# First projection of a two-MLP kernel: 384-column products, taken product by product over all of DFF

## The chip, the cores and the metric

The kernel runs on one core of a Trainium2 chip. The metric is device time in microseconds, the median of a few executions. One execution was also taken with the hardware profiler; its rows are the rows of this document. Engines are called as the profile calls them: PE (TensorE matmul), PEld (TensorE weight load), DVE (VectorE), ACT (ScalarE), POOL (GpSimd) and SP, which here only issues transfers (DMA).

## The reference

```python
# linear attention: q, k, v are (8, 8, 576, 64)
q_s = softmax(q, axis=-1); k_s = softmax(k, axis=2)
kv = einsum('bhsd,bhse->bhde', k_s, v)
attn = einsum('bhsd,bhde->bhse', q_s, kv)
x = attn.transpose(0, 2, 1, 3).reshape(4608, 512)
# first MLP: 512 -> 2048 -> 512
h = x @ w_in;  r = max(h, 0);  y = (r * r) @ w_out
# second MLP: 512 -> 2048 -> 512
h = y @ w2_in; out = (max(h, 0) + alpha * min(h, 0)) @ w2_out
```

All four matrix products have 4608 tokens; DFF is 2048 and the model width is 512.

## The kernel before

**Four stages.** The hidden stage of the first MLP (with the attention woven in) runs on nine tiles of 512 tokens, matmul line L759. It stores the squared hidden values to DRAM (`r_dram[0]`, L780). The first projection, `project_stage`, reads them back (L809), and stores its result to `y_scratch` (L877). The hidden stage of the second MLP, `hidden_wide`, reads that (L942, L945), runs at line L983 and stores to `r_dram[1]` (L1046). The second projection is `project_stage` again (matmul line L796 for both projections, output store L881).

**Split operands.** Every float32 operand is split into a head and a rest of type float32r (`split`: head by ACT at L484, rest by DVE at L487). Each product of operands is three matmuls: rest times head, head times rest, head times head (`PAIRS`).

**Seven products for eight.** Both projections and the wide hidden stage use Strassen's scheme with Winograd's sums: a 2x2 block product is made from seven products, numbered 1 to 7, of blocks and of sums of blocks. The sums of the weights are made once, behind the first hidden stage, and parked in DRAM (`made`, store L461). They come back when their stage begins (`brought`, load L465), one group `g` (256 of the 2048 rows of DFF) at a time, 896 KB each, all seven blocks of the group together.

**`project_stage`.** For each tile of 512 tokens and each of eight groups `g`, `token_blocks` loads four blocks of 256 tokens by 128 rows of DFF, makes the three sums on DVE (L503, L509, L512; in the last tile two of them on POOL), and splits everything: three blocks at once (768 columns) and twice two sums (512 columns). The group then does its seven products, each six matmuls of 256 columns (`product`). Each of the seven products has a PSUM bank of its own, which is summed over the eight groups. When the tile ends, `combine` makes the four result blocks from the seven banks on ACT and DVE (L828, L835, L844).

**`hidden_wide`.** Tiles are four times 512 tokens wide per half (1024 tokens) and once 256. Here banks are reused: product 6 is added to product 1's bank after ACT has copied it out, and so on (the `read` table in `Group.product`), with the copies and sums between products (L1005, L1008, L1035, L1011).

**What sets the order.** Python code adds operations to a `Plan` with an engine, an estimated cost, what they come after, and which buffers they take new or use. `Plan.run` then picks, engine by engine, what is issued next (earliest due among those that can start), finds a place in the two big SBUF areas (`sb`, float32; `sr`, float32r) by each kind's list of homes and its quota, and so fixes the order of every engine's instructions. On the chip each engine runs its list in that order, and waits at its head.

Of the kernel before, what the change touches and what calls it, by code (L numbers as in the profile page):

```python
# [18 lines left out]
P = 128  # L19
TOK = 512  # L20
WORDS = (53 * 256, 168 * 256)
# [3 lines left out]
HALF = 256  # L25

# [217 lines left out]
def linear_attention_two_mlps(  # L244
# [34 lines left out]
    r_dram = [dram.tile([T, P, NF, TOK], F32, name=f"r{n}") for n in range(2)]  # L279
# [3 lines left out]
    y_dram = y_dram.rearrange("t p c (h n) -> t p (c h) n", h=2)  # L283
# [21 lines left out]
    early = dict(within=(63 * KB_ // 2, 53 * KB_))  # L305
    x_early = dict(area=1, within=(64 * KB_, 158 * KB_), top=True)

    def homes(first, step, n):
# [10 lines left out]
        kvw=kind(2 * P, 2 * KB + 2, area=1, homes=homes(158, 1, 10)),  # L319
        q=kind(2 * R * D, 2, **early), qe=kind(2 * R * D, 2, **early), ke=kind(2 * KR * D, 2, **early),  # L320
        km=kind(2 * D, 2, **early), m=kind(GRAIN, 2, **early), rs=kind(GRAIN, 2, **early),
        mx=kind(GRAIN, 2, **early), sm=kind(GRAIN, 2, **early), ro=kind(2 * BANK, 2, **early),
        qT=kind(2 * BANK, 2, **x_early), x=kind(2 * BANK, 2 * KB + 2, **x_early),
        ri=kind(7 * HALF, 3, homes=homes(14, 7, 3)), o=kind(BANK, 8, homes=homes(37, 2, 8)),
        xr=kind(7 * BANK, 2, homes=homes(14, 14, 2)), xt=kind(2 * BANK, 14, area=1, homes=homes(112, 4, 14)),
        z=kind(2 * BANK, 8, homes=homes(49, -4, 2) + homes(8, -4, 3) + homes(38, -4, 7)),
        w3=kind(6 * HALF, G, area=1, homes=homes(0, 14, G)), w4=kind(8 * HALF, G, area=1, homes=homes(6, 14, G)),
        r3=kind(6 * HALF, 4, area=1, homes=homes(112, 6, 4)), r4=kind(4 * HALF, 8, area=1, homes=homes(136, 4, 8)),
# [90 lines left out]

    class Pairs:  # L420


        def __init__(self, n, kd, w, hidden, brought_after, signed=None):

            self.blocks, self.sums, self.done = [], [], []
            for g in range(G):
                t, f = hidden(g)
                made = self.made(n, kd, w, g, h1[t, f], begun[t] + 12 * MM * f + MADE, signed)
                self.brought(n, g, [made, brought_after[g]])
# [42 lines left out]

        def operand(self, g, p):

            s, i = A_OF[p]
            return [self.blocks, self.sums][s][g].ap.rearrange("p (n i m) -> p n i m", n=2, m=HALF)[:, :, i], s
# [244 lines left out]
    def hidden_stage(xs, weights, activate, store, blocks):  # L721
# [3 lines left out]
        stored = {}  # L725
        for t in range(T):
# [22 lines left out]
            for f in range(NF):  # L749
# [51 lines left out]
    def project_stage(r, stored, weights, first, store, gate):  # L801

        last, stored_c = {}, {}
        for t in range(T):

            acc = {p: bank(K["acc"]) for p in ((1, 2, 3, 6, 7, 4, 5) if first or t < T - 1 else (1, 6, 7, 5, 2, 3, 4))}
            for g in range(NF // 2):
                def load(to, t=t, g=g):
                    nc.sync.dma_start(to.rearrange("p (f t) -> p f t", f=2), r[t, :, 2 * g:2 * g + 2, :])  # L809
                bufs, done = token_blocks(load, [*stored[t, g], gate], t == T - 1)  # L810
# [64 lines left out]
    def store_y(t, i, j, c):  # L875
        to = y_dram[t].rearrange("p (k c h) n -> p k c h n", c=2, h=2)[:, 2 - i, :, 2 - j]
        nc.sync.dma_start(to, c.rearrange("p (c t) -> p c t", c=2))  # L877

# [6 lines left out]
    WIDE = [(t, BANK) for t in range(0, T - 1, 2)] + [(T - 1, HALF)]  # L885

    def wide_blocks(load, after, n):
# [27 lines left out]
        loaded = None  # L915
        for h in range(2):
            loaded = plan.add(
                lambda h=h: load(block(0, 4).rearrange("p (k h t) -> p k h t", k=2, h=2)[:, :, h], h), "sp", ISSUE,
                [*after, loaded], new=[] if h else [j], use=[j], mb=n / 1000,
            )  # L920
# [12 lines left out]
    def hidden_wide(weights, y_done, r, gate):  # L933

        last, stored = {}, {}
        for t, (first, n) in enumerate(WIDE):
            xs = []
            for c in range(2):
                def load(to, h, c=c, first=first, n=n):
                    if n == BANK:  # L940
                        y = y_dram[first + h].rearrange("p (k c h) t -> p k c (h t)", c=2, h=2)
                        nc.sync.dma_start(to, y[:, :, c])  # L942
                    else:
                        y = y_dram[first].rearrange("p (k c h) t -> p k c h t", c=2, h=2)
                        nc.sync.dma_start(to, y[:, :, c, h])  # L945
                ys = [y_done[t2, i, j] for t2 in range(first, first + n // HALF) for i in (1, 2) for j in (1, 2)]
                xs.append(wide_blocks(load, [*ys, gate(t, last)], n))
            for g in range(0, G, 2):
                both = [Group(weights, xs, t, first, n, g + m, r) for m in range(2)]
                for m, p in ((0, 1), (1, 1), (0, 2), (0, 6), (1, 6), (1, 2), (0, 5), (0, 7), (1, 7), (1, 5), (0, 4), (1, 4), (0, 3), (1, 3)):  # L950
                    last[t, g + m] = both[m].product(p)
                for m in range(2):
                    for h in range(2):
                        for t2 in range(first, first + n // HALF) if n == HALF else [first + h]:
                            stored.setdefault((t2, g + m), []).append(both[m].stored[h])
        return last, stored

    class Group:


        def __init__(self, weights, xs, t, first, n, g, r):
            self.weights, self.xs, self.first, self.n, self.g, self.r = weights, xs, first, n, g, r
            self.banks, self.ends, self.stored = {}, {}, {}
            self.z = [buf(K["z"]), buf(K["z"])]
# [5 lines left out]
        def product(self, p):  # L970
# [7 lines left out]
            def unit():  # L978
                a, _ = self.weights.operand(g, p)
                for c in range(2):  # L980
                    b = self.xs[c][0][p].ap.rearrange("p (n t) -> p n t", t=BANK if n == BANK else n)
                    for i, (u, w) in enumerate(PAIRS):
                        nc.tensor.matmul(  # L983
                            h.ap[:, :n], a[:, u, c * P:(c + 1) * P], b[:, w, :n],
# [6 lines left out]
            us = MM if n == BANK else MM2  # L991
            o = product_op(
                unit, 6 * us / MM, [self.weights.done[g][s], *(x[1][p] for x in self.xs), self.ends.get(read)],
# [47 lines left out]
        def store(self, h, after, z):  # L1041
            n, g, first = self.n, self.g, self.first

            def fn():
                to = self.r[first + h, :, 2 * g:2 * g + 2, :] if n == BANK else self.r[first, :, 2 * g:2 * g + 2, h * n:(h + 1) * n]
                nc.sync.dma_start(to, z.ap[:, :2 * n].rearrange("p (f t) -> p f t", f=2))  # L1046

            self.stored[h] = plan.add(fn, "sp", ISSUE, after, use=[z], due=now[0] + 8.0, mb=n / 1000)
# [29 lines left out]
    w1o = Pairs(0, "o", w1_out, lambda g: (1 + g // 4, 4 * (g % 4)), [h1[T - 1, max(0, 2 * (g - 3))] for g in range(G)])  # L1078
    p1, y_done = project_stage(r_dram[0], r1, w1o, True, store_y, h1[T - 1, 8])
    w2i = Pairs(1, "i", w2_in, lambda g: (3 + g // 4, 4 * (g % 4)), [p1[T - 1, max(0, g - 2), 5] for g in range(G)])  # L1080
    h2, r2 = hidden_wide(w2i, y_done, r_dram[1], lambda t, h2: p1[T - 1, 3, 5] if t == 0 else h2[t - 1, 3])
    end = len(WIDE) - 1
    w2o = Pairs(2, "o", w2_out, lambda g: (5 + g // 4, 4 * (g % 4)), [h2[end, max(0, g - 2)] for g in range(G)], signed)
# [31 lines left out]
```

## Time and profile before

| | |
|---|---|
| median of 3 runs | 1604.04 us (1603.2 to 1604.18) |
| the profiled execution | 1603.52 us, its span 1601.7 us |
| PE, DVE, ACT, POOL busy | 98%, 74%, 52%, 8% of the span |
| granted PE clock | 0.996 of full over the span |
| first hidden stage, first projection, wide hidden stage, second projection | end at 522.0, 886.4, 1234.4 and 1601.7 us |

Busy time is the union of an engine's instructions. Matmuls overlap one another, so the time that one costs in a stream is the stretch divided by the count, not the mean duration of one. A stretch in which PE is busy throughout can only become shorter through fewer or cheaper matmuls; a gap in it belongs to whoever PE waited for.

### The profile page before, as it was taken

To read this page: it belongs to the slowest core of one execution; us is meant where nothing else is said; L and a number is where in the kernel's file an instruction comes from. 1 tells how busy PE (TensorE), PEld (TensorE's weight loads), DVE (VectorE), ACT (ScalarE), POOL (GpSimd) and SP (SyncE) were. 2 spreads that over 40 slices of the span, in tenths; PEclk is the share of its full clock that TensorE was granted. 3 is DMA by queue.
4 is the path that set the end of the run, shared out by engine and by line. 5 is a ranking of instruction groups with operands and counts; after the bars stand their busy time and mean duration, and the time that the engine had idled before them with its cause. 6 is when DMAs were issued, how large, how long until landed. Compare 5 with 4: busy or idle time off the path is not lost.

```text
span 1601.7 us, 27016 instructions
## 1 busy us (share of the span) xinstructions
PE 1563.7 (98%) x10496; PEld 1418.2 (89%) x10496; DVE 1193.0 (74%) x2058; ACT 829.2 (52%) x1352; POOL 133.9 (8%) x140
## 2 busy tenths in 40 slices
PE   4899999999999999999999999999999999999998
PEld 3678888888888999999999788888889999999998
DVE  6766666677634888888877877768578998888873
ACT  5676766766657644444444543434246544444442
POOL 4440212011100000000012000000000000000012
PEclk9999999999999999999999999999999999999999
DMA  8667778888658544444445442434327554444431
GB/s 211 199 205 264 271 236 277 278 264 279 247 201 287 174 138 138 133 131 132 132 132 211 171 158 115 174 115 175 128 109 263 194 162 133 145 140 129 131 121 62
DMA packets 128976, 286.99 MB, mean 179 GB/s; under 512 B 15184, under 2 KB 78672, under 8 KB 128848
## 3 DMA queue, kind: packets, MB, share of 16 engines
q1 hardware_dynamic: 128848, 285.27, 54.1%
q8 instruction: 82, 1.34, 0.4%
q14 instruction: 46, 0.38, 0.1%
HBM read 168.83 MB, written 116.39 MB: 178 GB/s over the span
## 4 chain that ended last, share of the span: by engine, by line
PE 94%; DMA 2%; DVE 2%; issue 1%; POOL 1%; ACT 1%; SPq 0%; DVEq 0%; POOLq 0%
PE bank L796 45%; PE bank L759 23%; PE bank L983 21%; PE bank L593 1%; DMA sb<-in_moe_w_in_dram 1%; PE bank L667 1%; DMA sb<-in_k_dram 1%; PE bank L739 1%; PE bank L682 1%; PE bank L683 1%; PE bank L681 0%; POOL sr L400 0%; DMA sb<-in_q_dram 0%; DVE sr L487 0%; DVE sb L1011 0%
## 5 line engine op out<-in xcount | busy, mean ns | idle before, releaser
L796 PE MATMUL bank<-sr 128*128 128x256 f32 x6048 | 726.6, 283 | 0.4 <-DVE sr L487 0.4
L796 PEld LDWEIGHTS bank<-sr 128*128 128x128 f32 x6048 | 726.1, 192 | 0.8 <-DVE sr L487 0.6
L484 ACT CAST sr<-sb 128x512 fp32r<-128x512 f32 (+2 forms) x480 | 337.1, 718 | 357.6 <-PE bank L796 212.7
L487 DVE TENSOR_TENSOR sr<-sb,sr 128x512 fp32r<-128x512 f32 (+2 forms) x480 | 380.7, 818 | 108.8 <-ACT sr L484 107.6
L759 PE MATMUL bank<-sr 128*128 128x512 f32 x1680 | 406.9, 397 | 5.4 <-POOL sr L400 5.4
L759 PEld LDWEIGHTS bank<-sr 128*128 128x128 f32 x1680 | 312.1, 190 | 72.3 <-POOL sr L400 7.1
L983 PE MATMUL bank<-sr 128*128 128x512 f32 (+1 forms) x1680 | 346.4, 368 | 2.1 <-ACT sr L909 1.3
L983 PEld LDWEIGHTS bank<-sr 128*128 128x128 f32 x1680 | 293.0, 188 | 55.3 <-ACT sr L909 1.8
L1005 ACT ACTIVATE sb<-bank,sign 128x512 f32<-128x512 f32 (+1 forms) x160 | 103.4, 648 | 194.9 <-PE bank L983 190.2
L787 ACT ACTIVATE sb<-bank 128x512 f32<-128x512 f32 x144 | 85.8, 596 | 75.5 <-PE bank L759 64.9
L1011 DVE SCALAR_TENSOR_TENSOR sb<-sb,al 128x512 f32<-128x512 f32 (+1 forms) x160 | 110.0, 697 | 11.4 <-ACT sb L1005 8.0
L509 POOL TENSOR_TENSOR sb<-sb 128x256 f32<-128x256 f32 x16 | 16.7, 1045 | 1097.8 <-ACT sr L484 1060.3
L503 DVE TENSOR_TENSOR sb<-sb 128x512 f32<-128x512 f32 x144 | 100.1, 695 | 1.5 <-DMA sb<-r 1.5
L835 DVE TENSOR_TENSOR sb<-sb,bank 128x512 f32<-128x512 f32 x108 | 71.3, 686 | 35.1 <-PE bank L796 15.4
L788 ACT ACTIVATE sb<-sb 128x512 f32<-128x512 f32 x144 | 91.3, 634 | 3.4
L1008 DVE SCALAR_TENSOR_TENSOR sb<-bank,sign,sb 128x512 f32<-128x512 f32 (+1 forms) x80 | 55.5, 694 | 41.8 <-PE bank L983 39.6
L512 DVE TENSOR_TENSOR sb<-sb 128x256 f32<-128x256 f32 x128 | 54.3, 424 | 4.0
L663 POOL TENSOR_TENSOR sb<-sb 128x512 f32<-128x512 f32 x36 | 37.9, 1053 | 228.9 <-DVE sb L659 103.5
L509 DVE TENSOR_TENSOR sb<-sb 128x256 f32<-128x256 f32 x128 | 53.9, 421 | 0.7
L689 DVE TENSOR_TENSOR sr<-bank,sr 128x512 fp32r<-128x512 f32 x36 | 24.8, 690 | 37.2 <-ACT sr L686 36.9
L566 DVE TENSOR_REDUCE sb<-sb 128x128 f32<-128x640 f32 x32 | 41.6, 1301 | 9.4 <-DMA sb<-in_k_dram 7.0
L1035 DVE SCALAR_TENSOR_TENSOR sb<-bank,sign,sb 128x512 f32<-128x512 f32 (+1 forms) x40 | 27.7, 697 | 27.8 <-ACT sb L1005 20.2
(68 smaller groups left out, 913.4 us busy)
## 6 DMA issues: line engine op xcount, KB each, us to landing
sb<-r SPq DMA_DIRECT2D x144, 512.0 KB, 3.7
r<-sb SPq DMA_DIRECT2D x136, 512.0 KB, 3.0
j<-sb SPq DMA_DIRECT2D x24, 896.0 KB, 5.8
sb<-j SPq DMA_DIRECT2D x24, 896.0 KB, 5.8
sb<-in_moe_w_in_dram SPq DMA_DIRECT2D x32, 512.0 KB, 5.2
sb<-in_moe_w_out_dram SPq DMA_DIRECT2D x32, 512.0 KB, 4.6
y_scratch<-sb SPq DMA_DIRECT2D x36, 256.0 KB, 2.6
out_dram<-sb SPq DMA_DIRECT2D x36, 256.0 KB, 2.6
```

What stands on the lines that cost most here:

```text
L484: nc.scalar.copy(of(parts.ap[:, :n]), what())
L487: nc.vector.tensor_tensor(of(parts.ap[:, n:]), what(), of(parts.ap[:, :n].bitcast(F32)), op=ALU.subtract)
L503: nc.vector.tensor_tensor(two(block(4, 2)), two(block(1, 2)), block(0).unsqueeze(1).to_broadcast([P, 2, HALF]), op=ALU.subtract)
L509: e.tensor_tensor(block(6), block(2), block(4), op=ALU.add)
L759: nc.tensor.matmul(h.ap, w[:, a, c, :], x_parts(x[c][0])[:, b, :], start=(c == 0 and n == 0), stop=(c == KB - 1 and n == 2),)
L787: o = plan.add(lambda: nc.scalar.activation(ro.ap[:, half], h.ap, AF.Relu), "act", 0.6, [o, even], new=new, use=[h, ro])
L788: return plan.add(lambda: nc.scalar.activation(ro.ap[:, half], ro.ap[:, half], AF.Square), "act", 0.63, [o], use=[ro])
L796: nc.tensor.matmul(target[:, m * HALF:(m + 1) * HALF], one[:, u, ms], two[:, w, :], start=start and m == 0 and i == 0, stop=stop and m == ...
L835: lambda: nc.vector.tensor_tensor(c.ap, b.ap, acc[p].ap, op=ALU.add), "dve", 0.7,
L983: nc.tensor.matmul(h.ap[:, :n], a[:, u, c * P:(c + 1) * P], b[:, w, :n], start=start and c == 0 and i == 0, stop=c == 1 and i == 2, skip_g ...
L1005: nc.scalar.mul(to, h.ap[:, :n], sign[:, by])
L1011: nc.vector.scalar_tensor_tensor(to, to, al[:, by], to, op0=ALU.mult, op1=ALU.max)
```

## The change

The first projection gets a stage of its own, `project_wide`. A tile is now 768 tokens, six tiles in all, and a block is 384 tokens wide. The loop is turned inside out: for each of the seven products (in the order 1, 2, 5, 6, 7, 4, 3) all eight groups of DFF are run through before the next product, for both halves `m` of the output rows, in one PSUM bank for each half. The bank is carried from product to product as in `hidden_wide`, so that results leave it by a copy on ACT and three sums on DVE for each half and tile (class `Side`). The weights come back by product instead of by group: seven loads of 1 MB (`brought_all`), 256 columns out of each group, and one split of 2048 columns each. The tokens come as sixteen loads of 384 KB for a tile, the sums are made in place (`combine`), and the operands of a product stand in four slots of which there are eight.

Around it: `r_dram` and `y_scratch` are laid out by partition, so that a store or load of 512 tokens has runs of 2 KB instead of 4 KB; the wide hidden stage has four tiles of 464 tokens per half and one of 448; the second projection has 7 instead of 8 buffers for its sums (`r4`); `ro`, the two store buffers of the first hidden stage, have fixed places; SBUF is divided anew.

```diff
-WORDS = (53 * 256, 168 * 256)
+WORDS = (57 * 256, 164 * 256)
+WIDE = 464
+THIRD = 384
...
-    r_dram = [dram.tile([T, P, NF, TOK], F32, name=f"r{n}") for n in range(2)]
+    r_dram = [dram.tile([P, NF, NT], F32, name=f"r{n}") for n in range(2)]
...
+        pp=kind(2 * DFF // 2, 2, homes=homes(16, 8, 2)), wp=kind(2 * DFF, 4, area=1, homes=homes(0, 16, 4)), wq=kind(2 * DFF, 3, area=1, homes=homes(64, 16, 3)),
+        rb=kind(2 * THIRD, 16, homes=homes(33, 3, 5) + homes(0, 3, 11)), tt=kind(4 * THIRD, 8, area=1, homes=homes(112, 6, 8)),
+        c=kind(THIRD, 6, homes=homes(48, 1.5, 6)),
...
-        r3=kind(6 * HALF, 4, area=1, homes=homes(112, 6, 4)), r4=kind(4 * HALF, 8, area=1, homes=homes(136, 4, 8)),
+        r3=kind(6 * HALF, 4, area=1, homes=homes(112, 6, 4)), r4=kind(4 * HALF, 7, area=1, homes=homes(136, 4, 7)),
...
+    ORDER = (1, 2, 5, 6, 7, 4, 3)
...
+            if self.by_product:
+                self.all, self.done, self.loads = {}, {}, []
+                for i in (4, 5, 6, 0, 1, 2, 3):
+                    self.brought_all(self.n, ORDER[i], K["wp" if i < 4 else "wq"], [*self.parts, after[i]])
...
+    def project_wide(r, stored, weights, gate):
...
+        for t in range(NT // (2 * n)):
...
+            bring(1)
+            operand(1, 1)
+            bring(3)
+            operand(2, 3)
+            bring(0)
+            combine(1, 1, 0, ALU.subtract)
+            operand(5, 1)
+            bring(2)
+            combine(1, 2, 1, ALU.add)
+            operand(6, 1)
+            combine(0, 2, 0, ALU.subtract)
+            operand(7, 0)
+            combine(3, 3, 1, ALU.subtract)
+            operand(4, 3)
+            operand(3, 2)
+            sides = [Side(weights, slots, split_done, t, t0, n, m, y_done) for m in range(2)]
+            for p in ORDER:
+                for part in range(2):
+                    for m in range(2):
+                        for q in (2 * part, 2 * part + 1):
+                            last[t, p] = sides[m].product(p, q)
...
+            read = {6: 1, 7: 6, 4: 7, 3: 5}.get(p) if q == 0 else None
...
-    WIDE = [(t, BANK) for t in range(0, T - 1, 2)] + [(T - 1, HALF)]
+    WIDES = [(2 * WIDE * t, min(WIDE, NT // 2 - WIDE * t)) for t in range(-(-NT // (2 * WIDE)))]
...
+    w1o.bring([h1[T - 1, max(0, 4 * (i - 1))] if i < 4 else h1[T - 2, 8] for i in range(7)])
...
+    p1, y_done = project_wide(r_dram[0], r1, w1o, lambda t, p1, b: [p1[t - 1, 5]] if t else w1o_gate[b])
```

How the order of instructions moves, at three places. In the changed kernel L805 is the old L759 (first hidden stage), L1007 the matmul of the new stage, L826 the store of `r` (old L780), L508 the load of a product's weights, L494 the old L465, L942 the token load of the new stage, L533 the old L487, L952 the sums of token blocks and L1030 the sums from the banks.

PE at the end of the first hidden stage, before:

```order
L759 MATMUL bank_70<-sr 128x512 x12
L759 MATMUL bank_68<-sr 128x512 x12
L759 MATMUL bank_69<-sr 128x512 x12
L796 MATMUL bank_72<-sr 128x256 x6
L796 MATMUL bank_65<-sr 128x256 x6
L796 MATMUL bank_66<-sr 128x256 x6
```

and after:

```order
L805 MATMUL bank_71<-sr 128x512 x12
L1007 MATMUL bank_69<-sr 128x384 x12
L1007 MATMUL bank_70<-sr 128x384 x12
L1007 MATMUL bank_69<-sr 128x384 x6
L805 MATMUL bank_72<-sr 128x512 x12
L805 MATMUL bank_68<-sr 128x512 x12
L805 MATMUL bank_67<-sr 128x512 x12
L805 MATMUL bank_66<-sr 128x512 x12
L1007 MATMUL bank_69<-sr 128x384 x6
L1007 MATMUL bank_70<-sr 128x384 x12
```

Before, the projection began when the last hidden row block was through; now thirty of its 384-column matmuls stand ahead of the last four row blocks, and wait there for their operands.

SP in the last tile of the first hidden stage, before (`r` are the stores of hidden values and the token loads, `j` the parked weights):

```order
L461 DMA j_77<-sb 128x1792
L780 DMA r_73<-sb 128x1024 x2
L465 DMA sb<-j_75 128x1792 x2
L780 DMA r_73<-sb 128x1024 x2
L465 DMA sb<-j_75 128x1792
L780 DMA r_73<-sb 128x1024
L465 DMA sb<-j_75 128x1792
L780 DMA r_73<-sb 128x1024
L809 DMA sb<-r_73 128x1024 x2
L465 DMA sb<-j_75 128x1792
```

and after:

```order
L508 DMA sb<-j_75 128x8x256 x2
L826 DMA r_73<-sb 128x2x512
L490 DMA j_77<-sb 128x1792
L826 DMA r_73<-sb 128x2x512
L508 DMA sb<-j_75 128x8x256
L826 DMA r_73<-sb 128x2x512 x2
L508 DMA sb<-j_75 128x8x256 x2
L826 DMA r_73<-sb 128x2x512 x2
L942 DMA sb<-r_73 128x2x384 x8
L508 DMA sb<-j_75 128x8x256
L826 DMA r_73<-sb 128x2x512 x2
L508 DMA sb<-j_75 128x8x256
```

All seven weight loads now stand here, in runs of 1 KB (256 floats), and eight token loads in runs of 1.5 KB; before, the group loads stood here one by one between the stores, in one run of 7 KB for each partition, with token loads in runs of 4 KB.

DVE in the middle of the first projection, before (one group is one L503, L509, L512 and three L487):

```order
L487 TENSOR_TENSOR sr<-sb,sr 128x768
L509 TENSOR_TENSOR sb<-sb 128x256
L512 TENSOR_TENSOR sb<-sb 128x256
L487 TENSOR_TENSOR sr<-sb,sr 128x512 x2
L503 TENSOR_TENSOR sb<-sb 128x512
```

and after, some half of a tile:

```order
L533 TENSOR_TENSOR sr<-sb,sr 128x768 x2
L1030 TENSOR_TENSOR sb<-bank_65,sb 128x384
L952 TENSOR_TENSOR sb<-sb 128x768 x2
L1030 TENSOR_TENSOR sb<-bank_71,sb 128x384
L533 TENSOR_TENSOR sr<-sb,sr 128x768 x2
L952 TENSOR_TENSOR sb<-sb 128x768
L533 TENSOR_TENSOR sr<-sb,sr 128x768 x2
L952 TENSOR_TENSOR sb<-sb 128x768 x2
L533 TENSOR_TENSOR sr<-sb,sr 128x768 x8
L1030 TENSOR_TENSOR sb<-bank_72,sb 128x384
```

All splits and sums of blocks have 768 columns now, and the sums from the banks are spread over the tile instead of standing at its end.

## Rows read from the trace of the kernel before

**Rows 1.** The page, part 1: engine, busy us (share of the span), instructions.
```profile
PE 1563.7 (98%) x10496; PEld 1418.2 (89%) x10496; DVE 1193.0 (74%) x2058; ACT 829.2 (52%) x1352; POOL 133.9 (8%) x140
```
**Rows 2.** The page, part 4: the chain that ended last, shares of the span.
```profile
PE 94%; DMA 2%; DVE 2%; issue 1%; POOL 1%; ACT 1%; SPq 0%; DVEq 0%; POOLq 0%
PE bank L796 45%; PE bank L759 23%; PE bank L983 21%; PE bank L593 1%; DMA sb<-in_moe_w_in_dram 1%; PE bank L667 1%; DMA sb<-in_k_dram 1%; PE bank L739 1%; PE bank L682 1%; PE bank L683 1%; PE bank L681 0%; POOL sr L400 0%; DMA sb<-in_q_dram 0%; DVE sr L487 0%; DVE sb L1011 0%
```
**Rows 3.** Windows by stage: from:to, length, busy us (instructions), clock, DMA share, GB/s.
```profile
0.00:28.00 28.00, 9.43 (x59) 6.11 (x60) 17.86 (x39) 11.99 (x21) 12.38 (x26) 1.00 0.81 201
522.00:886.40 364.40, 363.56 (x3027) 363.09 (x3026) 301.44 (x480) 168.81 (x252) 16.14 (x16) 1.00 0.47 146
886.40:1234.40 348.00, 346.32 (x1685) 293.40 (x1686) 261.83 (x396) 148.71 (x243) 0.00 (x0) 1.00 0.42 154
1234.40:1601.70 367.30, 362.42 (x3019) 362.02 (x3017) 298.87 (x486) 162.02 (x240) 15.65 (x17) 1.00 0.45 139
```
**Rows 4.** Waits of PE from 500 us on: us in total, times, longest.
```profile
PE bank L983 <- ACT sr L909: 1.3, 1, 1.3
PE bank L983 <- DVE sr L911: 0.8, 1, 0.8
PE bank L796 <- DVE sr L487: 0.4, 1, 0.4
```
**Rows 5.** Timeline of PE in the first projection: start, us, line, count.
```profile
529.75 350.44 PE L796 MATMUL bank<-sr 128*128 128x256 f32 x2919
```
**Rows 6.** The chain in order of time, last matmuls of the first hidden stage.
```profile
475.75 46.24 PE bank L759 x204
```
**Rows 7.** Groups by line and form, 900 to 1100 us: busy us, mean ns.
```profile
L983 PE MATMUL bank<-sr 128*128 128x512 f32 x884 | 200.5, 389 | 0.0
```
**Rows 8.** Groups by line and form, whole span, DVE and ACT.
```profile
L487 DVE TENSOR_TENSOR sr<-sb,sr 128x768 fp32r<-128x768 f32 x168 | 160.7, 961 | 52.7 <-ACT sr L484 52.2
L484 ACT CAST sr<-sb 128x768 fp32r<-128x768 f32 x168 | 140.4, 837 | 155.3 <-PE bank L796 128.7 <-issue 10.1 <-DMA sb<-r 8.0
L835 DVE TENSOR_TENSOR sb<-sb,bank 128x512 f32<-128x512 f32 x108 | 71.3, 686 | 35.1 <-PE bank L796 15.4 <-ACT sb L828 15.1 <-DVE sb L844 0.5
L512 DVE TENSOR_TENSOR sb<-sb 128x256 f32<-128x256 f32 x128 | 54.3, 424 | 4.0
L828 ACT COPY sb<-bank 128x512 f32<-128x512 f32 x36 | 21.2, 589 | 34.6 <-PE bank L796 32.2 <-DMA sb<-r 1.6
L1005 ACT ACTIVATE sb<-bank,sign 128x512 f32<-128x512 f32 x128 | 88.4, 691 | 176.9 <-PE bank L983 176.8
```
**Rows 9.** The page, part 6: transfers, count, KB each, median us from issue to landing.
```profile
sb<-r SPq DMA_DIRECT2D x144, 512.0 KB, 3.7
r<-sb SPq DMA_DIRECT2D x136, 512.0 KB, 3.0
j<-sb SPq DMA_DIRECT2D x24, 896.0 KB, 5.8
sb<-in_moe_w_in_dram SPq DMA_DIRECT2D x32, 512.0 KB, 5.2
sb<-in_moe_w_out_dram SPq DMA_DIRECT2D x32, 512.0 KB, 4.6
sb<-y_scratch SPq DMA_DIRECT2D x16, 512.0 KB, 6.6
```
**Rows 10.** Windows at the end of the first hidden stage, columns as in rows 3.
```profile
459.40:522.00 62.60, 62.60 (x280) 51.83 (x280) 24.61 (x37) 40.97 (x65) 0.00 (x0) 1.00 0.64 231
480.00:522.00 42.00, 42.00 (x188) 34.80 (x187) 19.14 (x26) 30.31 (x46) 0.00 (x0) 1.00 0.79 278
```
**Rows 11.** Timeline at a tile's end in the second projection.
```profile
1311.08 0.69 DVE L835 TENSOR_TENSOR sb<-sb,bank 128x512 f32<-128x512 f32 x1 [1.42 <-ACT sb L828]
...
1324.03 0.62 ACT L484 CAST sr<-sb 128x512 fp32r<-128x512 f32 x1 [1.94 <-PE bank L796]
```
**Rows 12.** Window of the first hidden stage from 64 us on, columns as in rows 3.
```profile
64.00:522.00 458.00, 448.85 (x2510) 368.13 (x2511) 283.44 (x603) 313.29 (x555) 74.53 (x69) 0.99 0.75 255
```

More of the change, by code (lines that the diff above doesn't have):

```diff
@@ L471, in brought, with brought_all, load @@
             self.sums.append(sums)
+        def brought_all(self, n, p, kd, after):
+            j, parts = buf(K["pp"]), buf(kd)
+            s, i = A_OF[p]
+            i += 3 * s
+            def load():
+                nc.sync.dma_start(
+                    j.ap.rearrange("p (g m) -> p g m", g=G), j_dram[n].rearrange("g p m -> p g m")[:, :, i * HALF:(i + 1) * HALF]
+                )
+            o = plan.add(load, "sp", ISSUE, after, new=[j], mb=1.05)
+            self.loads.append(o)
+            self.done[p] = split(parts, lambda: j.ap, G * HALF, [o], [j])
+            self.all[p] = parts
         def operand(self, g, p):
+            if self.by_product:
+                return self.all[p].ap.rearrange("p (n g m) -> p n g m", n=2, g=G)[:, :, g], None
             s, i = A_OF[p]
@@ L724, in hidden_stage @@
         last = {}
-        stored = {}
+        stored = Stored()
         for t in range(T):
@@ L883, in store_out, with bring, load, combine @@
         )
-    WIDE = [(t, BANK) for t in range(0, T - 1, 2)] + [(T - 1, HALF)]
+    def project_wide(r, stored, weights, gate):
+        n = THIRD
+        last, y_done = {}, Stored()
+        for t in range(NT // (2 * n)):
+            t0 = 2 * n * t
+            raw, ready, slots, split_done = {}, {}, {}, {}
+            def bring(b):
+                k, h = divmod(b, 2)
+                for q in range(G // 2):
+                    x = buf(K["rb"])
+                    def load(x=x, q=q, t0=t0):
+                        of = r.rearrange("p (g k) t -> p g k t", k=2)[:, 2 * q:2 * q + 2, k, t0 + h * n:t0 + (h + 1) * n]
+                        nc.sync.dma_start(x.ap.rearrange("p (g t) -> p g t", g=2), of)
+                    after = [*stored.of(t0 + h * n, n, (2 * q, 2 * q + 1)), *gate(t, last, b)]
+                    raw[b, q] = x
+                    ready[b, q] = [plan.add(load, "sp", ISSUE, after, new=[x], mb=0.393)]
+            def combine(to, one, two, op):
+                for q in range(G // 2):
+                    x, y, z = raw[to, q], raw[one, q], raw[two, q]
+                    ready[to, q] = [plan.add(
+                        lambda x=x, y=y, z=z: nc.vector.tensor_tensor(x.ap, y.ap, z.ap, op=op), "dve", dve_us(2 * n),
+                        [*ready[to, q], *ready[one, q], *ready[two, q]], use=[x, y, z], lock=True,
+                    )]
+            def operand(p, b):
+                for q in range(G // 2):
+                    x, j = buf(K["tt"]), raw[b, q]
+                    slots[p, q] = x
+                    split_done[p, q] = split(x, lambda j=j: j.ap, 2 * n, ready[b, q], [j])
+                    ready[b, q] = [*ready[b, q], split_done[p, q]]
+            bring(1)
[19 more added lines that the diff above has]
+                            last[t, p] = sides[m].product(p, q)
+        return last, y_done
@@ L913, in operand @@
             )
[L915 to L920, printed above, removed]
+        loaded = plan.add(lambda: load(block(0, 4).rearrange("p (k t) -> p k t", k=2)), "sp", ISSUE, after, new=[j], mb=n / 500)
         sums = plan.add(t13, "dve", dve_us(2 * n), [loaded], use=[j], lock=True)
@@ L990, in product @@
             read = {6: 1, 7: 6, 4: 7, 3: 5}.get(p)
-            us = MM if n == BANK else MM2
             o = product_op(
-                unit, 6 * us / MM, [self.weights.done[g][s], *(x[1][p] for x in self.xs), self.ends.get(read)],
+                unit, 6 * (n / 2400 + 0.0133) / MM, [self.weights.done[g][s], *(x[1][p] for x in self.xs), self.ends.get(read)],
                 new=[h] if start else [], use=[h, wb, *(x[0][p] for x in self.xs)],
```

153 lines of the change are left out of this document (108 added, 45 removed).

## The prediction

> **What bounds the kernel now.** First the busy times: PE works in 98% of the span, DVE in 74% [rows 1]. The chain that ended last says the same: 94% of it is PE, and the matmul line of the two projections, L796, alone has 45% [rows 2]. Next the windows by stage. The reader is to see that the first projection, 364.4 us long, has PE busy for 363.6 of them, at a granted clock of 1.00, while DVE is busy for 301 and ACT for 169; the wide hidden stage and the second projection look alike, and the large PE gap is in the first 28 us, where PE works 9.4 [rows 3]. Last the waits: from 500 us on PE waited 2.5 us in three places, 2.1 of them at the beginning of the wide hidden stage [rows 4]. So in the stage that is changed nothing but the price and number of its matmuls counts, as long as no new wait arises.
>
> **The matmuls of the first projection.** In the steady stretch 2919 matmuls of 256 columns took 350.44 us, 0.1201 us each [rows 5]. The stage has 9 tiles x 8 groups x 7 products x 6 = 3024 of them: 363.0 us. At 512 columns 204 matmuls of the first hidden stage took 46.24 us, 0.2267 each [rows 6], and 884 of the wide hidden stage 200.5, 0.2268 each [rows 7]. So 256 columns more cost 0.1067 us, 0.4165 ns a column, and each matmul costs 0.1201 - 0.1066 = 0.0135 us beside its columns. The changed stage has 6 tiles x 7 products x 8 groups x 2 halves x 3 = 2016 matmuls of 384 columns: the same columns in two thirds of the instructions. No row has 384 columns in a stream. The ends are 0.1599 us (columns alone; 322.4 us, 40.6 less) and 0.2267 (as 512; 457 us, 94 more). I take the middle of the two measured widths, 0.1734, because the price beside the columns is the same at both: 2016 x 0.1734 = 349.5 us, **13.5 us less**. One ns on each would be 2 us.
>
> The Trainium skill, "TensorE: Matmul & The Clock Gate", section "Back-to-back issue gap", speaks against this size: it gives N/2.4 + 2.5 ns for an isolated stream at full clock, so that 1008 matmuls fewer would save 2.5 us and no more. This trace does not agree: by that rule 256 and 512 columns cost 109.2 and 215.8 ns, and the rows have 10.9 ns more at either width.
>
> **The wide hidden stage** keeps its 1680 matmuls and their columns: before 1344 of 512 and 336 of 256, 304.6 + 40.3 = 345.0 us; after 1344 of 464 (0.2067) and 336 of 448 (0.2000), 277.8 + 67.2 = 345.0. Nothing. The second projection keeps its 3024.
>
> **DVE and ACT inside the new stage.** A product of one tile is 48 matmuls, 8.32 us, a tile 58.2. Per tile DVE has 16 sums and 28 splits of 768 columns at 0.961, and six sums from banks of 384 columns between 0.424 (256 columns) and 0.686 (512), say 0.55 [rows 8]: 42.3 + 3.3 = 45.6 us. ACT has 28 heads at 0.837 and eight copies of at most 0.589 [rows 8]: 28.2 us. Both fit. The eight slots hold two products, so the splits of the next product can be made while this one runs, and the sums in place need no slot and run ahead of that. Product 7 is added to the bank that ACT has just copied product 6 out of. Between lie the twelve matmuls of the other half, 2.08 us, against a copy of 0.589 with at most one head of 0.837 ahead of it; in the wide hidden stage now a copy of 0.691 [rows 8] has twelve matmuls of 0.2267 as cover, and no wait is seen. I take 0; if the cover were gone it is at most 0.59 x 4 x 6 = 14 us.
>
> **The hand-over into the stage.** Seven weight loads move ahead on SP's queue, between the stores of `r`, and past them the eight token loads of the first two blocks. PE has thirty new matmuls ahead of its last four row blocks, and ACT has weight heads of 2048 columns (8/3 of 0.837, at most 2.2 us each) ahead of bank copies of the hidden stage. So whatever lands late stops the stores, their two buffers, ACT's copies and, by the banks, PE. From product 7's load (due after row block 8 of the last tile but one, 23 blocks of 2.72 us, 62.6 us before the end) I count on SP's list 7 x 1.05 MB of weights, ten stores of 0.52, one parked 0.92, eight tokens loads of 0.39: 16.6 MB. The trace moved 231 GB/s there, 14.5 MB, and 278 in the last 42 us [rows 10]; at 278 the 16.6 MB need 60 us. They fit with little to spare, if the shorter runs (1 and 1.5 KB for 10.5 of the MB) cost nothing. Two pairs of rows bound that: `w_in` (runs of 1 KB) lands in 5.2 us and `w_out` (4 KB) in 4.6, a factor 1.13; `y_scratch` (2 KB) lands in 6.6 and `r` (4 KB) in 3.7, a factor 1.8 [rows 9]. With 1.13: 10.5/0.246 + 6.1/0.278 = 65 us, 2.4 late, of which the weights of product 6 are not needed for another 25 us. I take **+1.5 us**, from -0 (PE has no wait here now) to +20 (below).
>
> **The hand-over out of it.** The first matmuls of the wide hidden stage need operands of both column halves, and all seven of the first half get their place before the second half gets one: eight places, while product 3 still holds four slots. Six places come free with product 4's slots, the rest in the middle of product 3, 4.2 us before the end. Head, rest and hand-over of one operand are some 1.5 us. I take the same 2.1 us wait as before, so 0; ends -2.1 and +4.
>
> **Second projection.** Seven buffers for sums instead of eight shorten the lead of DVE by half a group, 2.5 us of PE. At a tile's end DVE begins the sums from the banks at 1311.1 and ACT waits for PE's buffers again at 1324.0 [rows 11], so the lead is refilled within a third of a tile; I take **+0.5**, ends 0 and +4. Its loads and the stores of 464 columns have shorter runs; at a DMA share of 0.45 [rows 3] they have room.
>
> **First hidden stage.** With the fixed places of `ro`, the planner's order changes from about 64 us on. From there PE idles 458.0 - 448.85 = 9.2 us [rows 12]. Gone or doubled: ends -9 and +9; nothing says which, so 0.
>
> **Sum.** 1603.5 (the profiled execution, span and what lies around it) - 13.5 + 1.5 + 0.5 = 1592.0; the median of the runs stands 0.5 above the profiled one: **1592.5 us**.
>
> **Rivals.**
> - *Operands come no faster than they are used.* A product whose blocks are sums takes DVE 8 x 0.961 = 7.7 us, with two sums from banks 8.8, against PE's 8.32. If DVE can't run ahead, because tokens of the next tile have to wait for the sixteen buffers of this one, four products in each of six tiles cost 0.5 us: 12 us, and the time is 1604. For it: 45.6 of 58.2 us is a mean. Against: slots for two products, and buffers of the first blocks come free some 25 us before the next tile.
> - *Slower: the transfers at the hand-over.* If short runs cost the factor 1.8, the 10.5 MB go at 154 GB/s: 68 + 22 = 90 us for a window of 62.6, 28 late. Product 6's load (7 us) may be late; the rest, some 20 us, is a stall of PE ahead of the last four row blocks: 1592.5 + 20 - 1.5 = 1611. It decides from a lateness of 15 us on (a factor of about 1.45). Against: the 6.6 us of `y_scratch` are those of loads issued two at a time beside weight loads.
> - *The price goes with the columns alone.* If 0.1201 us for 256 is 0.469 ns a column here, 384 cost 0.180, the stage stays at 363 us, and the time is 1606. Against: the two widths that are measured. By the page's rule above it would be 2.5 us less.
> - *More than forecast:* 384 columns nearer to 0.170, or the gaps after 64 us go: 1580 to 1586.
>
> **How the numbers follow.** The forecast with its own ends (1586 to 1598) has 0.70, the supply of operands 0.10, late transfers 0.12 (half of it a partial stall), the price by columns 0.03, more than forecast 0.05. About 0.2% (3.2 us) is what a measurement can tell here. Faster: 0.70 + 0.05 + 0.02 + 0.03 of partial stalls = 0.80. Same, 1600.8 to 1607.2: 0.06 + 0.03 + 0.01 = 0.10. Slower: 0.02 + 0.06 + 0.02 = 0.10. Of the two outer sides I leave out 0.05 below 1585 and 0.12 above 1606.
>
> **What would show it.** Right: 2016 matmuls of the new line at 0.173 us each in a stretch without a gap, the stage 13 to 14 us shorter, the wide stage still 345 us of PE. Wrong: in PE's waits, a wait of the thirty early matmuls for a split of 2048 or 768 columns, or of row blocks for bank copies (transfers); many waits of some 0.5 us inside the stage for L533 (supply), or for the copies (product 6 to 7); a spacing of 0.180 (price).

## The result, and the profile after

The changed kernel takes **1588.07 us** (median of 4 runs, 1587.68 to 1588.73) against 1603.62 for the kernel before; the ratio is 0.9907 with a 95% interval of 0.989 to 0.9924. It is faster by 15.5 us, where 11.5 were forecast, and inside the range (1585 to 1606).

The profiled execution took 1588.73 us, its span is 1587.0. Its busy times answer to [rows 1]:

```profile
PE 1552.4 (98%) x9488; PEld 1425.0 (90%) x9488; DVE 1157.0 (73%) x1870; ACT 828.9 (52%) x1325; POOL 117.5 (7%) x124
```

PE has 1008 instructions fewer and is busy 11.3 us less. The windows by stage, with the same columns as [rows 3] (busy us of PE, PEld, DVE, ACT, POOL, then clock, DMA share, GB/s):

```profile
508.00:524.13 16.13, 16.13 (x79) 14.22 (x78) 5.17 (x4) 7.94 (x13) 0.00 (x0) 1.00 0.74 254
524.13:868.40 344.27, 344.27 (x1988) 344.26 (x1986) 270.35 (x314) 169.07 (x232) 0.00 (x0) 1.00 0.43 140
868.40:1219.10 350.70, 350.70 (x1681) 315.31 (x1681) 263.56 (x396) 150.55 (x244) 0.00 (x0) 1.00 0.45 159
1219.10:1587.00 367.90, 363.05 (x3025) 362.82 (x3024) 293.45 (x477) 157.72 (x236) 15.76 (x17) 1.00 0.44 132
```

PE is busy in the whole of every stretch but the last, where the last 4.9 us are the end of the program. The chain in order of time (start, us, line, count) shows the same without the tails of the matmuls; L805 is the first hidden stage, L1007 the first projection, L1141 the wide hidden stage, L842 the second projection:

```profile
470.07 38.08 PE bank L805 x168
508.15 5.22 PE bank L1007 x30
513.37 10.92 PE bank L805 x48
524.29 344.26 PE bank L1007 x1986
868.56 350.73 PE bank L1141 x1680
1219.29 362.87 PE bank L842 x3024
```

From 470 us to the last matmul no other engine stands in the chain. The waits of PE from 64 us on (us in total, times, longest) are all in the first hidden stage; the three of [rows 4] are gone:

```profile
PE bank L805 <- POOL sr L405: 4.2, 3, 2.0
PE bank L623 <- DVE sb L620: 2.0, 2, 1.6
```

The account of the 14.7 us between the two spans goes by the price of a matmul, from its start to the next one's start in the records of the traces.

- First projection: 3024 matmuls at 120.0 ns were 362.9 us, 2016 at 173.4 are 349.5 (5.22 + 344.26 in the chain). 13.4 less.
- Waits: beyond those prices PE lost 4.1 us from 472 us on before, and nothing now. 2.7 of them stood at the beginning of the wide hidden stage, 1.2 at its end and 0.3 in the second projection. [rows 4] has 2.5 of the 4.1, because PE counts as busy until its last matmul before a wait has ended.
- The first hidden stage ends at 524.29 - 5.22 = 519.1 instead of 522.0 us: 2.9 less.
- The wide hidden stage, which was to cost nothing, has become dearer. 464 columns cost 210.1 ns and 448 cost 203.6, where the straight line through 256 and 512 columns gave 206.7 and 200.0; before, 512 cost 226.7 and 256 cost 120.0, as on the line. 1344 x 210.1 + 336 x 203.6 ns is 350.7 us against 345.0: 5.7 more.

-13.4 - 4.1 - 2.9 + 5.7 is -14.7. The groups by form of the wide stage, after and then before (count, busy us, mean ns of one), show the same change from 346.6 to 351.1 us with the ends of matmuls ahead of waits counted in:

```profile
L1141 PE MATMUL bank<-sr 128*128 128x464 f32 x1344 | 282.5, 372 | 0.0
L1141 PE MATMUL bank<-sr 128*128 128x448 f32 x336 | 68.6, 366 | 0.0
```

```profile
L983 PE MATMUL bank<-sr 128*128 128x512 f32 x1344 | 305.4, 389 | 2.1 <-ACT sr L909 1.3 <-DVE sr L911 0.8
L983 PE MATMUL bank<-sr 128*128 128x256 f32 x336 | 41.2, 284 | 0.0
```

The transfers (count, KB, us to landing) answer to [rows 9]: the 72 stores of `r` in the first hidden stage, in runs of 2 KB instead of 4 KB, land in 4.1 us (first line), and at the hand-over nothing came of it.

```profile
r<-sb SPq DMA_DIRECT2D x72, 512.0 KB, 4.1
sb<-r SPq DMA_DIRECT2D x96, 384.0 KB, 4.5
sb<-r SPq DMA_DIRECT2D x72, 512.0 KB, 3.7
```

Before, the same 72 stores, at L780, had a median of 3.7 us; the 3.0 of [rows 9] is that of the stores of both hidden stages together.

```profile
DMA to landing us min/median/max: 2.6/3.7/9.4
```

### The profile page after: what moved, and what is told of

It is laid out like the page before. It is cut to its first block, busy times and chain, and to the rows that moved or that the text cites. A ratio compares the mean times of both kernels' runs of the same rounds, so it can differ in the third digit from the quotient of the medians.

```text
span 1587.0 us, 24824 instructions
## 1 busy us (share of the span) xinstructions
PE 1552.4 (98%) x9488; PEld 1425.0 (90%) x9488; DVE 1157.0 (73%) x1870; ACT 828.9 (52%) x1325; POOL 117.5 (7%) x124
## 4 chain that ended last, share of the span: by engine, by line
PE 95%; DMA 2%; DVE 1%; issue 1%; POOL 1%; ACT 0%; SPq 0%; DVEq 0%; POOLq 0%
PE bank L805 24%; PE bank L842 23%; PE bank L1141 22%; PE bank L1007 22%; PE bank L639 1%; PE bank L713 1%; DMA sb<-in_moe_w_in_dram 1%; PE bank L785 1%; PE bank L728 1%; PE bank L729 1%; PE bank L727 0%; POOL sr L405 0%; DMA sb<-in_q_dram 0%; DMA sb<-in_k_dram 0%; PE bank L617 0%
## 5 line engine op out<-in xcount | busy, mean ns | idle before, releaser
L530 ACT CAST sr<-sb 128x768 fp32r<-128x768 f32 (+3 forms) x423 | 327.1, 788 | 320.9 <-PE bank L842 125.7
L533 DVE TENSOR_TENSOR sr<-sb,sr 128x768 fp32r<-128x768 f32 (+3 forms) x423 | 373.7, 902 | 152.1 <-ACT sr L530 144.7
L805 PE MATMUL bank<-sr 128*128 128x512 f32 x1680 | 408.4, 398 | 4.6 <-POOL sr L405 4.5
L805 PEld LDWEIGHTS bank<-sr 128*128 128x128 f32 x1680 | 312.0, 190 | 71.9 <-POOL sr L405 6.2
L842 PEld LDWEIGHTS bank<-sr 128*128 128x128 f32 x3024 | 363.0, 192 | 0.0
L842 PE MATMUL bank<-sr 128*128 128x256 f32 x3024 | 363.0, 283 | 0.0
L1141 PE MATMUL bank<-sr 128*128 128x464 f32 (+1 forms) x1680 | 350.9, 371 | 0.0
L1007 PE MATMUL bank<-sr 128*128 128x384 f32 x2016 | 349.8, 334 | 0.0
L1007 PEld LDWEIGHTS bank<-sr 128*128 128x128 f32 x2016 | 349.5, 188 | 0.2
L1141 PEld LDWEIGHTS bank<-sr 128*128 128x128 f32 x1680 | 315.3, 188 | 35.4
L1162 ACT ACTIVATE sb<-bank,sign 128x464 f32<-128x464 f32 (+1 forms) x160 | 103.3, 646 | 197.1 <-PE bank L1141 181.9
L1168 DVE SCALAR_TENSOR_TENSOR sb<-sb,al 128x464 f32<-128x464 f32 (+1 forms) x160 | 110.6, 696 | 10.9 <-ACT sb L1162 7.3
L952 DVE TENSOR_TENSOR sb<-sb 128x768 f32<-128x768 f32 x96 | 88.4, 951 | 3.9 <-DMA sb<-r 3.5
L1165 DVE SCALAR_TENSOR_TENSOR sb<-bank,sign,sb 128x464 f32<-128x464 f32 (+1 forms) x80 | 55.5, 693 | 46.6 <-PE bank L1141 44.6
L549 DVE TENSOR_TENSOR sb<-sb 128x512 f32<-128x512 f32 x72 | 49.7, 691 | 0.0
L1192 DVE SCALAR_TENSOR_TENSOR sb<-bank,sign,sb 128x464 f32<-128x464 f32 (+1 forms) x40 | 27.9, 697 | 26.2 <-ACT sb L1162 17.7
```

Of the source, the lines that this page charges most:

```text
L530: nc.scalar.copy(of(parts.ap[:, :n]), what())
L533: nc.vector.tensor_tensor(of(parts.ap[:, n:]), what(), of(parts.ap[:, :n].bitcast(F32)), op=ALU.subtract)
L805: nc.tensor.matmul(h.ap, w[:, a, c, :], x_parts(x[c][0])[:, b, :], start=(c == 0 and n == 0), stop=(c == KB - 1 and n == 2),)
L842: nc.tensor.matmul(target[:, m * HALF:(m + 1) * HALF], one[:, u, ms], two[:, w, :], start=start and m == 0 and i == 0, stop=stop and m == ...
L952: lambda x=x, y=y, z=z: nc.vector.tensor_tensor(x.ap, y.ap, z.ap, op=op), "dve", dve_us(2 * n),
L1007: nc.tensor.matmul(h.ap[:, :n], a[:, u, ms], b[:, w, g], start=start and g == 0 and i == 0, stop=q == G // 2 - 1 and g == 1 and i == 2, sk ...
```

## The experiments

Two things were open. Is the gain that of fewer and wider matmuls, or of the new order and the banks? And why do 464 and 448 columns cost 3.4 and 3.6 ns more than the line, while 384 lies on it? (The expectations have 3.5 and 4.2, from busy time by count.) Three theories on the second: it is something in that stage (R), it is where the operands start in SBUF (A), or it is the width (W, B).

**e1: the wide stage at its old widths.**

```diff
-WORDS = (57 * 256, 164 * 256)
+WORDS = (53 * 256, 168 * 256)
...
-WIDE = 464
+WIDE = 512
...
-        rb=kind(2 * THIRD, 16, ...
+        rb=kind(2 * THIRD, 15, ...
-        c=kind(THIRD, 6, ...
+        c=kind(THIRD, 5, ...
...
-        r4=kind(4 * HALF, 7, ...
+        r4=kind(4 * HALF, 8, ...
```

The lines left out move the places of `ro`, of the attention's buffers and of the wide stage's operands to the new division of SBUF.

> The changed kernel with the wide hidden stage at 512 and 256 columns as in the kernel before (SBUF divided as before, one token buffer fewer in the first projection, one result buffer fewer, eight sum buffers in the second projection). In the changed kernel this stage took 350.7 us without a gap, 5.7 more than 345.0 by the straight line through 256, 384 and 512 columns: 464 columns cost 210.1 ns instead of 206.7, 448 cost 204.2 instead of 200.0. Theory W/A (464 and 448 columns, or where their operands start, cost more): 1680 matmuls take 345.0 us, the kernel 1588.1 - 5.7 = 1582.4, or up to 2.1 more if the wait at the beginning of the stage is back. Rival R (the stage is slower because of what runs beside it: shorter runs of the stores, other sums): 512 columns cost 230 ns here, the stage stays at 350, the kernel at 1588.

Measured: 1596.25 us, ratio to before 0.9963 (0.9949 to 0.9976), so 8.2 us slower than the changed kernel instead of 5.7 faster. The groups, and the waits of PE from 64 us on (all but those for POOL in the first hidden stage), say why:

```profile
L1141 PE MATMUL bank<-sr 128*128 128x512 f32 x1344 | 305.2, 389 | 0.0
L1141 PE MATMUL bank<-sr 128*128 128x256 f32 x336 | 42.2, 287 | 1.2 <-ACT sb L1162 1.2
```

```profile
PE bank L1007 <- ACT sr L530: 4.4, 1, 4.4
PE bank L623 <- DVE sb L620: 2.6, 2, 1.6
PE bank L1141 <- ACT sb L1162: 1.2, 1, 1.2
PE bank L842 <- DVE sr L533: 1.1, 2, 0.7
PE bank L1007 <- DVE sr L533: 0.5, 2, 0.3
```

The matmuls of the wide stage are back at their old price, 226.7 and 119.9 ns from one start to the next, so R falls. But at the hand-overs came waits of 7.2 us (all lines but that of L623). What was lost is more: 8.1 us in the first projection, 1.9 in the wide stage and 3.9 in the second projection, 13.8 in all, since the granted clock fell behind the waits (0.50 from 556.2 to 560 us); less the 5.7 gained, that is 8.1 of the 8.2. The transfers were not full when the first of these waits came (DMA share 0.56 from 500 to 524 us, 0.50 from 524 to 545). Buffers and places differ from the changed kernel together, and which of them brings the waits is not shown. So in these two layouts 464 columns go with hand-overs without a wait, and 512 with hand-overs that cost more than the width gains.

**e2: blocks of 256 columns, all else as changed.**

```diff
-THIRD = 384
+THIRD = 256
```

> The changed kernel with blocks of 256 columns and tiles of 512 tokens in the first projection: product by product, weights by product, sums in banks all stay, only the width goes back. Theory N (the stage became shorter because there are 1008 matmuls fewer, 13.5 ns each): 3024 matmuls at 0.120 us, 363.0 us for the stage, 13.5 more than the changed kernel, 1601.6 us. Rival L (it is the order, the banks or the spread of the sums that made it shorter): the stage stays near 350 us and the kernel near 1588. If operands come no faster than used at this size (DVE 44 x 0.70 + 6 x 0.42 = 33 of 40.3 us a tile), waits come on top.

Measured: 1608.81 us, ratio to before 1.0038 (1.0024 to 1.0053): the whole gain is gone, and more.

```profile
L1007 PE MATMUL bank<-sr 128*128 128x256 f32 x3024 | 363.5, 283 | 0.3 <-DVE sr L533 0.3
L1141 PE MATMUL bank<-sr 128*128 128x464 f32 x1344 | 285.0, 374 | 3.9 <-ACT sr L1082 3.2 <-DVE sr L1084 0.7
```

The stage takes 363 us again, 120.0 ns from one start to the next, with the new order and the new banks: N holds, L falls. Of the other 7.3 of the 20.7 us, 6.3 were lost at the way out: waits of 3.9 us, and behind them matmuls of 464 columns at the lower clock, 387 ns each instead of 210:

```profile
889.00:892.40 3.40, 3.40 (x10) 2.96 (x9) 2.71 (x4) 1.08 (x2) 0.00 (x0) 0.50 0.00 0
```

So these waits cost more than their length: behind them PE ran for a time at the lower of its two clock levels (1.2 instead of 2.4 GHz, a granted clock of 0.50). The waits of 1.3 and 0.8 us at the same place in the kernel before left the clock at 1.00:

```profile
886.00:892.00 6.00, 4.29 (x18) 3.33 (x19) 6.00 (x10) 5.14 (x9) 0.00 (x0) 1.00 0.28 90
```

**e3, e6 and e7: the operands of the first projection moved by 128, 256 and 384 bytes.**

```diff
-tt=kind(4 * THIRD, 8, area=1, homes=homes(112, 6, 8)),
+tt=kind(4 * THIRD, 8, area=1, homes=homes(112.125, 6, 8)),
```

(112.25 and 112.375 in the other two.)

> The changed kernel with the operand slots of the first projection moved by 128 bytes, so that every 384-column operand starts 128 bytes behind a 512-byte boundary, as most operands of 464 columns do in the wide stage. Theory A (the start of the operand costs): a 384-column matmul goes from 173.4 ns to some 177, the stage from 349.5 to 356.5 us. Theory W (the width costs): 173.4 ns, 349.5 us as before.

> The changed kernel with the operand slots of the first projection moved by 256 bytes. With 128 bytes a 384-column matmul took 175.6 ns instead of 173.4. Theory A1 (any start off a 512-byte boundary costs the same): 175.6 ns, 353.9 us for 2016. Theory A2 (the cost grows with the distance from the boundary): 177 to 178 ns, 357 to 359 us, and the 4.2 ns of the 448-column tile, whose rests start 256 bytes behind a boundary, are explained in part. Theory A3 (256 bytes is a boundary too): 173.4 ns.

> As the run before, moved by 384 bytes. A1: 175.6 ns. A2: 179 to 180 ns. A3: 175.6 ns, as at 128 bytes.

The long stretch of the stage in the chain of each, in this order:

```profile
524.58 348.65 PE bank L1007 x1986
```

```profile
524.89 344.26 PE bank L1007 x1986
```

```profile
524.18 348.65 PE bank L1007 x1986
```

At 128 and 384 bytes a matmul takes 348.65/1986 = 0.1756 us, 2.2 ns more than the 0.1733 at 0 and at 256. So A3: a moving operand that starts on a 256-byte boundary costs nothing more, one that starts 128 bytes off does, 4.4 us for the stage. This is a cause, but too small. In the wide stage the slots lie 3.625 KB apart, so at 464 columns two thirds of the moving operands start off such a boundary (all rests, by 64 or 192 bytes, which no run measured, and every second head), and at 448 half of them. At 2.2 ns each that makes an estimated 1.5 and 1.1 ns of a surplus of 3.4 and 3.6.

**e4: 320 of 384 columns.** The rest of each block is left out.

```diff
-h.ap[:, :n], a[:, u, ms], b[:, w, g],
+h.ap[:, :320], a[:, u, ms], b[:, w, g, :320],
```

> The changed kernel with the matmuls of the first projection cut to 320 of the 384 columns (the last 64 tokens of each block are left out, so its output is not the reference's); operands start where they did. 320 is 2.5 times 128, as 448 is 3.5 times. By the straight line a matmul costs 0.1467 us, the stage 295.8 us. Theory W (a width that is no multiple of 128 costs 4 ns more): 0.151 us, 304 us. Theory A (only the start costs): 0.1467 us. If operands come later than PE uses them (46 of 49 us of DVE a tile), PE has gaps; the spacing is then read from stretches without one.

```profile
542.44 271.15 PE bank L1007 x1847
```

271.15/1847 = 0.1468 us against 0.1467 by the line: 320 columns cost nothing more, and W in its first form (any width that is no multiple of 128) falls.

**e5: the wide stage in six tiles of 384 columns.**

```diff
-WIDE = 464
+WIDE = 384
...
-xt=kind(2 * WIDE, 14, area=1, homes=homes(112, 3.625, 14)),
+xt=kind(2 * WIDE, 14, area=1, homes=homes(112, 3, 14)),
```

> The changed kernel with the wide hidden stage in six tiles of 384 columns per half, every operand on a 512-byte boundary (places 3 KB apart). Theory A (464 and 448 columns were dear because their operands start off the boundary): 2016 matmuls at 0.1734 us, 349.5 us for the stage against 350.7 in spite of 336 matmuls more; the kernel 1588.1 - 1.2 = 1586.9. Rival R (something else in that stage adds 3 to 4 ns to each matmul): 0.1768 us each, 356.4 us, the kernel at 1594. A new wait at the sixth tile's beginning could hide either; then the spacing in stretches without a gap decides.

Measured: 1588.15 us, ratio to before 0.9912 (0.9898 to 0.9925), the same as the changed kernel.

```profile
868.37 349.44 PE bank L1141 x2016
1217.81 27.60 PE bank L842 x231
1245.40 1.99 issue
```

The stage is 1.3 us shorter with 336 matmuls more, 0.1733 each, as on the line: nothing else in that stage raises the price of a matmul, and R falls again; width and start changed together here. The second projection then lost 0.8 us near its beginning, where the chain leaves PE.

**e8: three weight loads later.**

```diff
-w1o.bring([... if i < 4 else h1[T - 2, 8] for i in range(7)])
+w1o.bring([... if i < 4 else h1[T - 1, 0] for i in range(7)])
```

> The changed kernel with the first three weight loads of the first projection (products 7, 4 and 3) asked for after the first row block of the last tile instead of after the ninth of the last tile but one, 8 row blocks or 21.8 us later; the planner places the rest anew. It tests whether the transfers at the hand-over stand at their limit, as the slower rival of the prediction had it. Limit (the 16.6 MB need 60 us): the last loads come some 20 us late, PE waits some 10 us or more in front of the first 384-column matmuls, or the hidden stage's last row blocks wait for their bank copies. Room (transfers had time to spare): PE waits less than 3 us and the first projection ends within 3 us of 868.4 us.

```profile
480.00:522.00 42.00, 42.00 (x192) 35.49 (x191) 15.11 (x9) 28.25 (x37) 0.00 (x0) 1.00 0.96 321
522.00:545.00 23.00, 20.09 (x100) 19.37 (x99) 17.68 (x18) 13.01 (x17) 0.00 (x0) 0.85 0.56 178
```

It lies between the two expectations: PE waits 2.9 us and loses 6.1, and the stage ends at 873.56, 5.0 us later (the hidden stage before it had ended 1.1 us earlier), since the clock fell behind the wait here as well (0.85 on the mean; 320 ns for 384 columns where it was 0.50). The transfers took the squeeze by going to 321 GB/s at a DMA share of 0.96; the changed kernel has 289 GB/s at 0.85 in its last 42 us before 524. So there was room, but little of it: the slower rival of the prediction had the right place, and the rates that the prediction worked with there, 278 GB/s and for short runs 154, were too low.

**e9: the price of a width by itself.** The columns behind the width are left out.

```diff
+cols = (448, 464, 416, 480)[f // 4] if c or n else BANK
...
-h.ap, w[:, a, c, :], x_parts(x[c][0])[:, b, :],
+h.ap[:, :cols], w[:, a, c, :], x_parts(x[c][0])[:, b, :cols],
```

> The changed kernel with the matmuls of the first hidden stage cut in width: eleven of the twelve of each row block move 448 columns (row blocks 0 to 3), 464 (4 to 7), 416 (8 to 11) or 480 (12 to 15) instead of 512, so that its output is not the reference's; all operands start on a 512-byte boundary. It measures the price of a width by itself. By the straight line through 256, 384 and 512: 200.0, 206.7, 186.7 and 213.3 ns. Theory A (only the start of the operands costs): these, read as a unit of twelve less one matmul of 226.7 ns. Theory B (some widths cost more whatever the start; the wide stage had 204.2 and 210.1): 448 and 464 lie 3 to 4 ns above the line here too, and 416 and 480 show which widths do.

The last four row blocks, 480 columns, stand by themselves in the chain:

```profile
476.87 10.48 PE bank L806 x48
```

44 x 217.2 ns at 480 columns and 4 x 230.5 at 512 make up the 10.48 us.

In the last tile of tokens the changed kernel shows what undisturbed 512-column matmuls cost there: 226.7 ns (38.08 us for 168 in its chain above). In e9 the means from one start to the next in that tile are 204.1 ns for 448 columns, 209.3 for 464, 188.5 for 416 and 217.2 for 480 (43 or 44 of each): 4.1, 2.6, 1.8 and 3.9 above the line, all with operands on a 512-byte boundary. Over all tiles the means are 203.8, 209.2, 188.2 and 217.1, but there 512 columns cost 228.8 in the changed kernel too, so the last tile is the cleaner witness. So B: these widths cost more by themselves. One thing stays open: the one matmul of 512 columns among eleven narrower ones takes 227 to 236 ns, 231.5 on the mean, and the first twelve behind the early 384-column ones in the changed kernel 230.1 on the mean, so a part of the price may lie in the change from one width to another.

**e10: 448 columns in the wide stage of e1.** Here too the columns behind the width are left out.

```diff
-h.ap[:, :n], a[:, u, c * P:(c + 1) * P], b[:, w],
+h.ap[:, :min(n, 448)], a[:, u, c * P:(c + 1) * P], b[:, w, :min(n, 448)],
```

> The first of these kernels (wide hidden stage at 512 columns, operands 4 KB apart, all starts on a 512-byte boundary) with its 1344 wide matmuls cut to 448 of the 512 columns; the last 64 columns of each block are left out, so its output is not the reference's. Theory B (448 columns cost more by themselves): 203.8 ns each, as in the run of widths, 273.9 us for the 1344. Theory A (only starts off a 256-byte boundary cost): 200.0 ns, 268.8 us.

```profile
L1141 PE MATMUL bank<-sr 128*128 128x448 f32 x1344 | 273.1, 366 | 1.5 <-ACT sb L1162 1.3 <-DVE sr L1084 0.2
```

273.1/1344 = 0.2032 us with the waits' edges, and 202.7 ns from one start to the next: 2.7 above the line in a stream of one width, with every start on a boundary. B again, in the stage in question. Of the surplus of the changed kernel's wide stage, 5.7 us above the line, e9's prices make 1344 x 2.6 + 336 x 4.1 ns = 4.9. The remaining 0.8 us is less than the 2.3 that e3's price would make of the starts, so the two do not simply add, and how they share the price at 464 columns is not shown.

## Why the prediction was right

**The matmuls of the first projection: right, in size too.** 349.5 us were forecast and 349.48 are measured; e2 takes the width back and the 13.4 us go with it. The straight line between two measured widths held at 384 and, by e4, at 320. The Trainium skill's 2.5 ns beside the columns ("TensorE: Matmul & The Clock Gate", "Back-to-back issue gap"), by which 2.5 us would have been saved, is not what these runs show: at 256, 320, 384 and 512 columns it is 13.3 to 13.4 ns. The Trainium skill gives it there for an isolated matmul; here it is a stream with a weight load for each.

**The wide hidden stage: the step that failed.** It was put at nothing, by the same line read at 464 and 448, where no row stood. It cost 5.7 us more than that (e9, e10: the widths; e3, e7: the starts, in a share that is open). It is the one term that came out dearer than forecast, and without it the sum would have been further off than it was.

**The hand-over in: mis-sized.** +1.5 us were forecast, and there is no wait: the thirty early matmuls and the last four row blocks run without a gap. The limit of 278 GB/s was no limit (289 here, 321 in e8). That little was left shows in e8. In e1 a wait of 4.4 us came back at a DMA share of 0.50 to 0.56, so something other than the rate of transfers can stop this hand-over as well.

**The hand-over out, and the second projection.** 0 and +0.5 were taken; the 4.1 us that the waits of [rows 4] had cost, edges included, went. Four kernels tell with what: at the way out PE waited 2.1 us before (256-column blocks, 512-column wide tiles) and 3.9 in e2 (256, 464), but not in e1 (384, 512) nor in the changed kernel (384, 464). So the wait went with the 384-column blocks and not with the tiles of 464, though buffers differ among the four as well.

**The first hidden stage.** 0 was taken; it ends 2.9 us earlier. In five kernels whose instructions up to there stand in the same order (the changed one, e3, e4, e6, e7) the same 168 matmuls begin between 467.48 and 470.67 us:

```profile
467.48 38.08 PE bank L805 x168
```

```profile
470.67 38.08 PE bank L805 x168
```

So 3.2 us are the spread from one execution to the next, which is more than the 2.9. All ten profiles with the new first stage at full width end it 2.3 to 5.5 us before the one profile of the kernel before, which points at a gain; but with one profile on that side it is not shown, nor whether the new order or the fixed places of `ro` would have brought it. This stays open.

**The rivals.** Supply of operands: no wait inside the stage, DVE busy 270 of 344 us; its sums of 384 columns take 0.553 us and the copies of ACT 0.480, by

```profile
L1030 DVE TENSOR_TENSOR sb<-bank,sb 128x384 f32<-128x384 f32 x36 | 19.9, 553 | 5.8 <-ACT sb L1026 3.5 <-PE bank L1007 2.1
L1026 ACT COPY sb<-bank 128x384 f32<-128x384 f32 x48 | 23.1, 480 | 33.2 <-PE bank L1007 32.6 <-DMA sb<-r 0.3
```

(0.55 and at most 0.589 were put in). Late transfers: not here; 2.9 us of waits in e8, where three loads were asked for 21.8 us later. The price by columns alone: refuted by the spacing of 0.1733.

The forecast of 1592.5 was 4.4 us above the result: 1.5 + 0.5 of waits that did not come, 4.1 of waits that went and 2.9 of the first stage, less 5.7 of the wide stage, is 3.3; another 0.5 was added for the medians, and the changed kernel's median lies 0.7 below its profiled execution. So the direction and the main term, 13.4 of the 14.7 us, were right for the reason given, and that the sum came as near as 4.4 us is in part luck: errors of 9.0 us one way and 5.7 the other cancelled.

No version here beats the changed kernel: e5 equals it. One with the 512-column wide stage and without the waits of e1 would be an estimated 5 us faster by the prices above; whether a layout allows it is open.

## What to carry to other kernels

Where PE has no gap, count matmuls: each costs a fixed 13.3 ns here beside its columns at full clock, so blocks of 384 instead of 256 columns are worth almost 4% of a stage, if operands, banks and transfers can be arranged without a new wait. Don't read a price off a line at a width that no row has: measure it, and put moving operands on 256-byte boundaries. A wait at a hand-over can cost more than its length, since the clock can fall behind it: 3.9 us of waits cost 6.3 in e2, and 2.9 cost 6.1 in e8.

## What the runs showed of the hardware

- Start to start, float32r matmuls with weights loaded for each, at a granted clock of 1.00: 256 columns 120.0 ns, 320 146.7, 384 173.4, 512 226.7, all N/2.4 + 13.3 to 13.4; but 416 188.5, 448 202.7 to 204.1, 464 209.3 and 480 217.2, which is 1.8 to 4.1 ns more. Why these four and not 320 is not known.
- The same at a granted clock of 0.50: 256 columns 213 ns (e1), 384 320 (e1, e8) and 464 387 (e2), which is N/1.2 with nothing beside. The fixed 13.3 ns shows at the higher level alone.
- A moving operand that starts 128 or 384 bytes off a 512-byte boundary: 2.2 ns more at 384 columns; 256 bytes off: nothing.
- Transfers: 321 GB/s over 42 us at a DMA share of 0.96 (e8), with much of it in runs of 1 to 2 KB.
